# Attention in an order written out by hand: new engine orders and PSUM banks, with GpSimd's scaling and VectorE's work on weight words kept apart

## The chip, the cores and the metric

The kernel runs on one core of a Trainium2 chip. Five engines have queues of their own: TensorE (PE; its weight loads are PEld), VectorE (DVE), ScalarE (ACT), GpSimd (POOL) and SyncE (SP, which issues most DMAs). They work side by side and wait for one another by semaphores. The metric is the device time of one execution in microseconds, the lower the better.

## The reference, cut to what matters

Causal attention on 24 heads (2 batches of 12), then an ELU feed-forward, then a maxout feed-forward:

```python
scores = scale * (q @ k.T); scores = where(mask, -1e9, scores)   # (2, 12, 448, 448), head_dim 64
attn = softmax(scores); x = attn @ v                             # -> (896, 768)
h = x @ w_in; g = where(h > 0, h, exp(min(h, 0)) - 1)            # w_in (768, 2048)
x = g @ w_out                                                    # w_out (2048, 768)
h = maximum(maximum(x @ w1, x @ w2), x @ w3)                     # each (768, 768)
return (h @ w_out2).astype(float32)
```

## The kernel before, in words

The weights arrive as float64 words. Each is turned into float32 from its two 32-bit halves and then split into a high and a low part, so that one product is made of three matmuls (high by high, high by low, low by high).

Attention works on 12 pairs of heads, numbered 0 to B. Pairs 0 to 5 are the first batch (token half 0), pairs 6 to B the second (token half 1). Every step has a letter, and its digits are the pair, then the head or group:

- PE: `Q` transposes q or k (`qk_pe`, L196), `S` makes the scores (`s_pe`, L234), `T` transposes the weights of attention (`t_pe`, L297), `A` multiplies by v (`av_pe`, L322), `D` is an early part of `x @ w_in` for the first two blocks of w_in (`d_pe`, L357). The digits behind a colon are the PSUM banks (0 to 7) that the step takes.
- DVE: `M` adds the mask and takes the row maximum (`s_max`, L254), `I` adds a constant to the row sums and inverts them (`r_inv`, L280 and L281), `Y` is the low part of x (`x_lo`, L339), `f` and `k` finish the early g, and `b`, `c`, `l` work on a block of w_in: `b` shifts a word (`d_shift`, L406), `c` joins words in two instructions (`d_join`, through `join`, L99 and L100), `l` makes the low part (`d_lo`, L416).
- ACT: `E` is the exponential (`s_exp`, L268), `X` the high part of x (`x_hi`, L333), `a` and `h` work on w_in (`d_scale` L402, `d_hi` L413), `e` and `g` on the early g.
- DVE or ACT, as the table says: `K` copies transposed q or k out of PSUM (`qk_copy`), `C` copies the transposed weights (`t_copy`; L314 on DVE, L312 on ACT).
- POOL: `N` scales one piece of the weights by the inverted sum (`e_norm`, L287), four pieces to a head. A `T` step needs two to four of them.

The order is not found by a scheduler. `PLAN` (from L454) writes down, for each engine, the order of all its steps, and the loop below it issues them inside `tc.manual_schedule()` (L572), each once what it needs has been issued. On the chip an engine then works strictly through its own line and waits at each step for the results it reads and for the bank it writes. A bank is free when the step that reads it last (`holds`, L546) is done; for `A` that is the pair's `X` and `Y`.

After the table the dense part begins (L606). Its first unit is block 0 of w_in on token half 1: `h_unit(0, ...)` runs 18 matmuls (`ph`, L357) in the order of the pairs 6, 7, 8, 9, A, B, three for each: the high part of x, the low part, the high part. Then come block 1, and from block 2 on both halves; the second feed-forward follows (`py`, L723; `bx`, `by`, `bz`, L781), then the last product (L1049).

Of the kernel before, what the change touches and what calls it, by code (L numbers as in the profile page):

```python
# [31 lines left out]
def tile_attention_elu_maxout(  # L32
# [413 lines left out]
    def spin(n):  # L446
        for _ in range(n):
# [8 lines left out]
            L0 L1 L2 L3 V0 V1 R0 L4 R1 L5 V2 L6 V3 L7 V4 L8 V5 L9 R2 V6 LA V7 LB V8 V9 VA VB  # L456
            """,
        "PE": """
            Q00:0 Q01:1 S02:23 S00:45 S01:67 Q11:0 Q10:1 Q21:3 Q20:2 S11:46 S12:01 S10:57 S22:32
            S20:41 S21:05 Q31:7 Q30:3 T001:2 T002:4 T000:7 T010:5 T012:3 T011:1 S32:75 S31:34  # L460
            S30:12 A0:6 Q40:0 T100:2 Q41:3 T101:1 T111:4 T110:5 T112:0 T102:2 S42:37 S40:14
            S41:50 A1:2 T202:7 Q50:1 T201:5 Q51:0 Q61:3 T211:4 T210:5 T212:2 Q60:7 T200:3 T312:5
            T310:1 Q71:0 T300:2 T311:6 T301:4 T302:1 S52:32 S60:75 S61:60 S51:32 S50:41 A2:5
            A3:2 T410:4 Q81:6 Q70:7 T402:1 T412:0 T400:5 T401:3 T411:6 S62:75 S72:14 S71:36
            S70:75 A4:0 D00:4 T610:1 Q90:2 T511:6 D01 T512:0 T510:7 Q80:6 T611:5 T612:2 D02
            QA0:3 Q91:1 T500:0 D03 T600:7 T501:6 T502:3 T601:0 T602:7 S82:21 S81:30 S92:67
            S91:12 S90:57 S80:63 A5:0 A6:6 D04 T700:5 D05 T711:3 T710:7 T712:0 T702:2 QB0:5
            QB1:6 T701:7 T802:4 T810:5 QA1:0 T812:7 T801:2 T811:6 T800:5 SB2:04 SA2:32 SB0:16
            SA0:74 SB1:32 SA1:05 A7:1 A8:4 D10:7 T900:3 T902:0 T901:6 D11 T912:2 T910:0 T911:3
            D12 TB01:6 A9:0 D13 D14 D15 TB02:2 TB00:3 TB10:4 TA02:5 TA01:1 TA00:2 TB12:4 TB11:6  # L470
            TA11:3 TA12:7 TA10:4 AB:6 AA:2
            """,
        "DVE": """
            K00 M011 M001 M003 M000 M002 K11 M010 M013 M012 I00 M102 M100 M111 M101 M103 M113
            I01 M201 M211 M203 M212 M210 M213 C000 M110 C002 C001 M112 M202 M200 I10 M302 M310
            M313 M300 I11 M303 M312 M311 K40 K41 M301 I21 I20 C110 C112 C102 b0 M400 M410 M411
            M403 M402 M412 I31 M401 I30 M413 Y1 K61 C210 K51 Y0 C310 C200 C300 c0 M501 M511 C301
            M600 M613 M500 M510 M512 I41 M503 I40 M602 M603 M610 M513 M612 Y2 M502 b1 K70 C400
            C410 C411 M601 M611 I51 M710 M702 I61 l0 M711 M701 Y3 I50 M712 Y4 M703 I60 M713 M700
            c1 C510 K80 KA0 C600 C612 C502 C501 M811 M801 M800 M810 M911 M901 M802 M812 I71 I70  # L480
            M803 M903 M813 I80 M910 M913 Y5 M912 I81 C700 Y6 C710 M902 f0 C712 C702 C810 KA1
            C711 M900 l1 MB11 MA01 MA11 MB01 C800 MB03 MA13 I90 I91 k0 MB00 MA03 MB02 MA00 MA02
            MA10 MB13 IB0 MB12 MB10 C902 C900 C901 IA0 C910 C911 IB1 Y8 MA12 Y7 IA1 b2 CB02 CB01
            f1 CB12 CA00 CA10 CA02 CA12 k1 Y9 YB YA c2 l2
            """,
        "ACT": """
            K01 E011 E001 E003 E000 K10 E002 K21 K20 E013 E010 E012 E101 E111 E100 E113 K31 K30
            E103 C010 C012 C011 E212 E102 E210 E110 E112 E202 E200 E203 E213 C100 E211 E201 C101
            C111 E311 E310 E300 E313 E302 E301 E410 E312 E303 X0 X1 C201 C202 E413 K50 C212 C211
            a0 K60 C312 C311 K71 E411 E412 C302 E403 E401 E400 h0 E402 E500 E511 E613 E510 X2  # L490
            E600 E501 E512 K81 E513 C402 C401 E610 E612 C412 E611 E602 E503 X3 E502 E601 X4 E603
            a1 C511 K90 E712 C610 E701 C512 E703 h1 C500 E713 K91 C601 C602 E711 E710 C611 E801
            E702 E800 E901 E700 E811 E812 E802 E803 E810 X5 E813 E913 E912 X6 e0 a2 KB0 C701
            E911 KB1 C802 C801 C811 E910 C812 E900 g0 E903 EB11 E902 EB03 EA11 EA01 EA03 EB01
            EB00 EB02 EA02 EA10 EB12 EA00 X8 EB13 EB10 C912 EA13 EA12 X7 e1 CB10 CB00 CB11 g1 X9
            CA11 CA01 XB XA h2
            """,
        "POOL": """
            N001 N002 N003 N000 N012 N010 N013 N011 N101 N103 N102 N111 N112 N113 N110 N100 N201
            N200 N211 N203 N212 N210 N202 N213 N311 N312 N303 N310 N313 N302 N300 N301 N412 N411  # L500
            N413 N403 N402 N401 N410 N400 N510 N512 N613 N511 N612 N513 N500 N611 N610 N503 N600
            N603 N601 N602 N502 N501 N712 N702 N701 N710 N703 N713 N803 N802 N711 N700 N813 N801
            N810 N812 N800 N811 N911 N901 N910 N903 N900 N913 N902 N912 NB01 NB02 NB00 NB03 NA02
            NB13 NA03 NA00 NB10 NB12 NA01 NA13 NB11 NA10 NA12 NA11
            """,
    }

# [155 lines left out]
    with tc.manual_schedule():  # L663
# [375 lines left out]
        def bank4(name):  # L1039
            kinds.append(kinds.pop(0))  # L1040
            return bank3(kinds[-1], name)[:, :DMO]
# [49 lines left out]
        l1 = bank4("l1")  # L1091
# [50 lines left out]
        l2 = bank4("l2")  # L1142
# [47 lines left out]
```

## Time and profile before

| | |
|---|---|
| median of 3 runs | 481.5 us (481.31 to 481.86) |
| the profiled execution | 481.89 us |
| its span, first to last instruction | 480.1 us |
| attention: first transpose to the end of the last `A` | 4.78 to 97.87 us |
| PE busy | 473.9 us, 99% of the span |
| DVE, ACT, POOL busy | 387.5, 315.5, 50.2 us |
| granted TensorE clock | 1.000 over the span |

A row of a view has a start and a duration in microseconds, the engine, the line of the kernel, the instruction with what it writes and reads, its shape, and in brackets how long its engine had been idle and who released it. Busy time counts overlapping records once: matmuls are pipelined, and one record reaches into the next.

### The profile page before, as it was taken

To read this page: it belongs to the slowest core of one execution; us is meant where nothing else is said; L and a number is where in the kernel's file an instruction comes from. 1 tells how busy PE (TensorE), PEld (TensorE's weight loads), DVE (VectorE), ACT (ScalarE), POOL (GpSimd) and SP (SyncE) were. 2 spreads that over 40 slices of the span, in tenths; PEclk is the share of its full clock that TensorE was granted. 3 is DMA by queue.
4 is the path that set the end of the run, shared out by engine and by line. 5 is a ranking of instruction groups with operands and counts; after the bars stand their busy time and mean duration, and the time that the engine had idled before them with its cause. 6 is when DMAs were issued, how large, how long until landed. Compare 5 with 4: busy or idle time off the path is not lost.

```text
span 480.1 us, 7494 instructions
## 1 busy us (share of the span) xinstructions
PE 473.9 (99%) x2674; PEld 416.5 (87%) x2674; DVE 387.5 (81%) x757; ACT 315.5 (66%) x647; POOL 50.2 (10%) x104
## 2 busy tenths in 40 slices
PE   8999999999999999999999999999999999999997
PEld 5776777789998899988998899889999999999996
DVE  4999989768988888656776765698888878988985
ACT  4999899668998888655575745564555544535530
POOL 1673764500000000000000000000000000000000
PEclk9999999999999999999999999999999999999999
DMA  9999310027758765217775777631444432000104
GB/s 184 245 204 244 106 42 1 2 67 229 237 173 277 242 200 187 88 48 246 248 248 187 236 244 260 209 125 66 132 131 133 131 125 73 1 0 2 41 26 164
DMA packets 81653, 69.69 MB, mean 145 GB/s; under 512 B 35152, under 2 KB 75472, under 8 KB 81616
## 3 DMA queue, kind: packets, MB, share of 16 engines
q1 hardware_dynamic: 80544, 68.89, 49.3%
q8 instruction: 21, 0.34, 0.3%
q10 hardware_dynamic: 1072, 0.33, 0.3%
q14 instruction: 16, 0.13, 0.1%
HBM read 59.38 MB, written 9.83 MB: 144 GB/s over the span
## 4 chain that ended last, share of the span: by engine, by line
PE 96%; POOL 2%; DVE 1%; issue 0%; ACT 0%; POOLq 0%; DVEq 0%
PE py L723 24%; PE ph L357 24%; PE bx L781 14%; PE by L781 7%; PE s L234 5%; PE te L297 4%; PE av L322 4%; PE bz L781 3%; PE bzf L1049 3%; PE bxf L1049 2%; POOL e L287 2%; PE byf L1049 2%; PE bxl L1049 1%; PE tk L196 1%; PE tq L196 1%; PE idle L448 1%
## 5 line engine op out<-in xcount | busy, mean ns | idle before, releaser
L357 PE MATMUL ph<-x,ws_l 128*128 128x512 f32 (+2 forms) x576 | 118.6, 365 | 0.0
L723 PE MATMUL py<-gs,ws_o 128*128 128x512 f32 (+1 forms) x576 | 116.2, 363 | 0.0
L357 PEld LDWEIGHTS ph<-x,ws_l 128*128 128x128 f32 x576 | 103.9, 188 | 12.4 <-issue 1.0
L723 PEld LDWEIGHTS py<-gs,ws_o 128*128 128x128 f32 x576 | 104.3, 188 | 11.7
L287 POOL TENSOR_SCALAR e<-e,r 112x336 f32<-112x336 f32 (+3 forms) x96 | 48.9, 528 | 41.5 <-DVE r L281 40.8
L268 ACT ACTIVATE e<-e,nm 112x448 f32<-112x448 f32 (+3 forms) x96 | 49.9, 532 | 2.7 <-DVE nm L254 2.5
L254 DVE CUSTOM_DVE_ANT_0 e<-s,mask 112x224 f32<-112x224 f32 (+3 forms) x96 | 37.9, 441 | 2.4 <-PE s L234 2.3
L137 ACT ACTIVATE ws_o<-c_o 128x512 fp32r<-128x512 f32 x24 | 15.2, 632 | 36.3 <-PE py L723 36.3
L781 PE MATMUL by<-ops_s,wb 128*128 128x448 f32 x162 | 35.8, 365 | 0.0
L138 DVE TENSOR_TENSOR ws_o<-c_o,ws_o 128x512 fp32r<-128x512 f32 x24 | 16.6, 693 | 19.9 <-ACT ws_o L137 19.8
L781 PEld LDWEIGHTS by<-ops_s,wb 128*128 128x128 f32 x162 | 30.5, 188 | 2.4
L297 PE MATMUL te<-ident,e 112*112 112x112 f32 x240 | 27.5, 261 | 1.3 <-POOL e L287 1.2
L297 PEld LDWEIGHTS te<-ident,e 112*112 112x112 f32 x240 | 23.9, 134 | 3.7 <-POOL e L287 2.0
L661 ACT ACTIVATE u<-bx 128x448 f32<-128x448 f32 x9 | 4.9, 545 | 32.9 <-PE bx L781 32.9
L234 PE MATMUL s<-qk 64*112 64x224 f32 (+3 forms) x192 | 24.9, 405 | 0.2 <-ACT qk L211 0.2
L322 PE MATMUL av<-et,vn 112*64 112x448 f32 (+3 forms) x192 | 24.4, 404 | 0.0
L99 DVE SCALAR_TENSOR_TENSOR c_o<-c_o,raw_o 128x512 uint32<-128x512 uint32 x24 | 16.6, 693 | 9.5 <-ACT raw_o L95 8.7
L99 DVE SCALAR_TENSOR_TENSOR ce<-ce,raw_e 128x768 uint32<-128x768 uint32 x18 | 17.3, 958 | 7.1 <-ACT raw_e L95 7.1
L322 PEld LDWEIGHTS av<-et,vn 112*64 112x64 f32 x192 | 12.0, 137 | 12.4 <-issue 5.6
L137 ACT ACTIVATE gs<-g 128x512 fp32r<-128x512 f32 (+2 forms) x30 | 17.3, 577 | 7.6 <-DVE g L373 7.5
L234 PEld LDWEIGHTS s<-qk 64*112 64x112 f32 x192 | 16.1, 173 | 6.9 <-issue 1.5
L138 DVE TENSOR_TENSOR gs<-g,gs 128x512 fp32r<-128x512 f32 (+2 forms) x30 | 18.6, 621 | 4.1 <-ACT gs L137 4.0
(169 smaller groups left out, 870.7 us busy)
## 6 DMA issues: line engine op xcount, KB each, us to landing
raw_e<-in_moe_w_dram SPq DMA_DIRECT2D x18, 768.0 KB, 4.9
raw_l<-in_moe_w_in_dram SPq DMA_DIRECT2D x16, 768.0 KB, 5.4
raw_o<-in_moe_w_out_dram SPq DMA_DIRECT2D x24, 512.0 KB, 3.6
turned<-ce SPq DMA_DIRECT2D x18, 384.0 KB, 2.7
quad<-turned SPq DMA_DIRECT2D x18, 384.0 KB, 4.1
wx<-in_moe_w_out_dram SPq DMA_DIRECT2D x12, 384.0 KB, 3.1
qn<-in_q_dram SPq DMA_DIRECT2D x24, 112.0 KB, 4.2
vn<-in_v_dram SPq DMA_DIRECT2D x12, 224.0 KB, 4.4
```

Of the source, the lines that this page charges most:

```text
L99: nc.vector.scalar_tensor_tensor(r, r, 3, low, ALU.logical_shift_left, ALU.bitwise_or)
L138: nc.vector.tensor_tensor(lo, src, f32(hi), ALU.subtract)
L234: nc.tensor.matmul(s[j][:C, o : o + (c + 1) * C], qk[:, a, c * C : (c + 1) * C], qk[:, c2, : (c + 1) * C], start=(w == 0 and n == 0), stop ...
L254: nc.vector.tensor_tensor_reduce(out=e_t[h][:, EOFF[c] : EOFF[c] + (c + 1) * C], in0=ps_now.pop(("s", h, c)), in1=mask[:, (NCH - 1 - c) * ...
L268: nc.scalar.activation(e, e, AF.Exp, bias=nm_t[h][:, c : c + 1], scale=-1.0, accum_out=sm_t[p][:, j, c : c + 1],)
L287: nc.gpsimd.tensor_scalar(e, e, ps_now["r", h][:, c : c + 1], 1.0, ALU.mult, ALU.mult)
L297: nc.tensor.transpose(t[:C, n : n + C], e[:, EOFF[c] + j * C : EOFF[c] + (j + 1) * C], ident[:C, :C],)
L322: nc.tensor.matmul(a[j * D : (j + 1) * D, kc * C : S], vn[:, j * NCH + kc, :], et[j][:, TOFF[kc] : TOFF[kc] + S - kc * C], start=(n == 0), ...
L357: nc.tensor.matmul(ps, w(a, kc), x(c, kc), start=(i == 0), stop=(i == len(seq) - 1))
L723: nc.tensor.matmul(py[m, b][:, : at.stop - at.start], w[:, a, kc * P : (kc + 1) * P], g_sp[hk * HK + kc][:, c, at], start=(hk == 0 and i = ...
L781: nc.tensor.matmul(bank[:, :S], w, side[:, c, k, :], start=(not onto and k == 0 and (a, c) == (0, 0)), stop=(k == K2 - 1 and (a, c) == (1, ...
L1049: nc.tensor.matmul(out, a(x, k)[:, rows], b(y, k), start=begin and n == 0, stop=end and n == len(seq) - 1,)
```

## The change

Only `PLAN` changes (and one blank line goes, so that lines behind it move up by one). The steps are the same; the order of each engine but SP is new, PE's steps have other banks, and 27 copies (23 `C`, 4 `K`) go from DVE to ACT while 17 (11 `C`, 6 `K`) go the other way, so that DVE has 183 steps (193 before) and ACT 176 (166). In making the new orders, a scaling step of POOL and a step of DVE on words or blocks of weights were taken as never running at the same time. The last lines of four of the tables:

```diff
         "PE": """
...
-            D12 TB01:6 A9:0 D13 D14 D15 TB02:2 TB00:3 TB10:4 TA02:5 TA01:1 TA00:2 TB12:4 TB11:6
-            TA11:3 TA12:7 TA10:4 AB:6 AA:2
+            A7:7 A8:1 D10:6 T910:4 T900:0 T911:3 T902:2 T901:4 T912:0 D05 D11 A9:2 D12 TA01:3
+            TB10:0 TB11:4 TB12:5 D13 D14 TB02:0 TB01:4 TB00:5 D15 TA02:3 TA00:1 TA11:0 TA10:5
+            TA12:4 AB:3 AA:5
         "DVE": """
...
-            f1 CB12 CA00 CA10 CA02 CA12 k1 Y9 YB YA c2 l2
+            IB1 IB0 C910 C902 IA0 C912 f0 IA1 Y8 CB02 k0 b2 CA10 CA12 f1 k1 YB c2 l2 YA Y9 Y7
         "ACT": """
...
-            EB00 EB02 EA02 EA10 EB12 EA00 X8 EB13 EB10 C912 EA13 EA12 X7 e1 CB10 CB00 CB11 g1 X9
-            CA11 CA01 XB XA h2
+            EA11 g0 CB10 CB11 CB12 X8 CA01 CB00 X9 CB01 CA02 e1 CA11 CA00 g1 XB XA h2 X7
         "POOL": """
...
```

The first place is VectorE's join of block 1 of w_in (`c1`) about the middle of attention. Before, it stands behind the work on pairs 6 and 7, and the rows are these (`e14`, `e15` are heads of pair 7, `r12` and `et11` heads of pairs 6 and 5):

```order
L280 TENSOR_SCALAR r12_932<-sm6_704 112x4
L281 RECIPROCAL r12_932<-r12_932 112x4
L254 ISA e15_857,nm15_858<-s15_0_873,mask_79 112x448
L254 ISA nm15_858 112x1
L254 ISA e14_861,nm14_862<-s14_1_846,mask_79 112x112
L254 ISA nm14_862 112x1
L99 SCALAR_TENSOR_TENSOR c_l1_898<-c_l1_898,raw_l1_157 128x768
L100 SCALAR_TENSOR_TENSOR c_l1_898<-raw_l1_157,c_l1_898 128x768
L314 COPY et11_939<-te11_0_958 112x224
L213 TENSOR_SCALAR qk8_804<-tq8_961 128x448
```

The same place of the order after:

```order
L339 TENSOR_TENSOR x1_59<-av4_860,x0_58 128x448
L213 TENSOR_SCALAR qk9_957<-tq9_925 128x448
L213 TENSOR_SCALAR qk8_959<-tq8_933 128x448
L215 COPY qk9_957<-tk9_938 128x448
L314 COPY et13_999<-te13_2_968 112x448
L99 SCALAR_TENSOR_TENSOR c_l1_847<-c_l1_847,raw_l1_157 128x768
L100 SCALAR_TENSOR_TENSOR c_l1_847<-raw_l1_157,c_l1_847 128x768
L314 COPY et11_1032<-te11_0_1010 112x224
L254 ISA e16_1034,nm16_1035<-s16_2_1028,mask_79 112x224
```

The join no longer follows directly on the inverted sums of pair 6; it stands behind the copy of a transposed piece of pair 6 (`et13`), that is, behind a step that needs all four scalings of that head.

The second place is the end of VectorE's line and of ScalarE's in attention (`x1_59` and `x0_58` are the low and high parts of x, `av7` to `av11` the products of pairs 7 to B, `c_l2` and `ws_l2` block 2 of w_in). VectorE before:

```order
L440 TENSOR_TENSOR gs1_1526<-g_1_0_1520,gs1_1526 128x448
L339 TENSOR_TENSOR x1_59<-av9_1444,x0_58 128x448
L339 TENSOR_TENSOR x1_59<-av11_1540,x0_58 128x448
L339 TENSOR_TENSOR x1_59<-av10_1555,x0_58 128x448
L99 SCALAR_TENSOR_TENSOR c_l2_1199<-c_l2_1199,raw_l2_589 128x768
L100 SCALAR_TENSOR_TENSOR c_l2_1199<-raw_l2_589,c_l2_1199 128x768
L416 TENSOR_TENSOR ws_l2_1569<-c_l2_1199,ws_l2_1569 128x768
```

VectorE after:

```order
L440 TENSOR_TENSOR gs1_1548<-g_1_0_1544,gs1_1548 128x448
L339 TENSOR_TENSOR x1_59<-av11_1532,x0_58 128x448
L99 SCALAR_TENSOR_TENSOR c_l2_1306<-c_l2_1306,raw_l2_611 128x768
L100 SCALAR_TENSOR_TENSOR c_l2_1306<-raw_l2_611,c_l2_1306 128x768
L416 TENSOR_TENSOR ws_l2_1565<-c_l2_1306,ws_l2_1565 128x768
L339 TENSOR_TENSOR x1_59<-av10_1551,x0_58 128x448
L339 TENSOR_TENSOR x1_59<-av9_1428,x0_58 128x448
L339 TENSOR_TENSOR x1_59<-av7_1319,x0_58 128x448
```

ScalarE after, at the same place (before, the high part of pair 7 stood eight rows ahead of the high part of pair B):

```order
L436 ACTIVATE gs1_1548<-g_1_0_1544 128x448
L333 ACTIVATE x0_58<-av11_1532 128x448
L333 ACTIVATE x0_58<-av10_1551 128x448
L413 ACTIVATE ws_l2_1565<-c_l2_1306 128x768
L333 ACTIVATE x0_58<-av7_1319 128x448
```

The join and split of block 2 have moved ahead of the low parts of pairs A, 9 and 7, and pair 7 is now the last of all.

The third place is PE's step from attention to the dense part, with the semaphores that a row waits for (PE before, then PE after):

```order
L322 MATMUL av10_1555<-et20_1523,vn10_1122 64x224
L322 MATMUL av10_1555<-et21_1529,vn10_1122 64x224
L357 MATMUL ph0_0_1585<-x0_58,ws_l0_713 128x448 [waits PE_49]
L357 MATMUL ph0_0_1585<-x1_59,ws_l0_713 128x448
L357 MATMUL ph0_0_1585<-x0_58,ws_l0_713 128x448 x2
L357 MATMUL ph0_0_1585<-x1_59,ws_l0_713 128x448
L357 MATMUL ph0_0_1585<-x0_58,ws_l0_713 128x448 x2
L357 MATMUL ph0_0_1585<-x1_59,ws_l0_713 128x448
```

```order
L322 MATMUL av10_1551<-et20_1491,vn10_1137 64x224 [waits Activation_49]
L322 MATMUL av10_1551<-et21_1541,vn10_1137 64x224
L357 MATMUL ph0_0_1585<-x0_58,ws_l0_696 128x448 [waits DVE_49]
L357 MATMUL ph0_0_1585<-x1_59,ws_l0_696 128x448
L357 MATMUL ph0_0_1585<-x0_58,ws_l0_696 128x448
L357 MATMUL ph0_0_1585<-x0_58,ws_l0_696 128x448 [waits Activation_49]
L357 MATMUL ph0_0_1585<-x1_59,ws_l0_696 128x448
L357 MATMUL ph0_0_1585<-x0_58,ws_l0_696 128x448 x2
```

The order of PE's rows is the same; the first matmul of the dense part now waits for VectorE, and the fourth, which reads pair 7's high part, for ScalarE.

## Rows read from the trace of the kernel before

**Rows 1.** The page: span, then busy time of each engine.

```profile
span 480.1 us, 7494 instructions
PE 473.9 (99%) x2674; PEld 416.5 (87%) x2674; DVE 387.5 (81%) x757; ACT 315.5 (66%) x647; POOL 50.2 (10%) x104
```

**Rows 2.** Chain of waits, 98 us to the end: start, duration, engine and line.

```profile
97.87 108.79 PE ph L357 x540
206.66 116.00 PE py L723 x576
```

**Rows 3.** Windows: length, busy by engine (instructions), granted clock, DMA share, GB/s.

```profile
10.00:48.00 38.00, 37.89 (x331) 27.69 (x331) 36.60 (x154) 37.91 (x129) 20.52 (x42) 1.00 1.15 230
48.00:58.00 10.00, 8.82 (x68) 6.82 (x69) 9.22 (x28) 8.79 (x26) 8.93 (x15) 1.00 0.28 62
58.00:98.00 40.00, 40.00 (x332) 29.36 (x330) 33.91 (x120) 33.07 (x105) 19.43 (x40) 1.00 0.11 30
```

**Rows 4.** Chain of waits, 0 to 98 us.

```profile
1.19 3.60 PE idle L448 x8
4.78 0.93 PE tq L196 x4
...
6.99 2.15 PE s L234 x16
...
9.68 0.38 PE tq L196 x4
...
21.88 1.59 POOL e L287 x3
...
23.52 1.36 PE te L297 x12
...
48.67 8.27 POOL e L287 x13
...
93.95 3.92 PE av L322 x32
```

**Rows 5.** Timeline, 44 to 60 us.

```profile
53.41 1.46 DVE L99 SCALAR_TENSOR_TENSOR c_l<-c_l,raw_l 128x768 uint32<-128x768 uint32 x1
...
54.90 1.09 DVE L100 SCALAR_TENSOR_TENSOR c_l<-raw_l,c_l 128x768 uint32<-128x768 uint32 x1
...
56.98 0.40 PE L297 MATMUL te<-ident,e 112*112 112x112 f32 x2 [1.18 <-POOL e L287]
```

**Rows 6.** Timeline of POOL, 0 to 100 us.

```profile
48.67 8.69 POOL L287 TENSOR_SCALAR e<-e,r 112x448 f32<-112x448 f32 x14 [0.43 <-DVE r L281]
...
64.65 7.17 POOL L287 TENSOR_SCALAR e<-e,r 112x336 f32<-112x336 f32 x15 [0.43 <-DVE r L281]
```

**Rows 7.** Line L280, all instructions: duration in ns, min/median/max.

```profile
L280 DVE TENSOR_SCALAR r<-sm x24: 140/172/524, 11.5 to 89.0; 112x4 f32<-112x4 f32 x24
```

**Rows 8.** Timeline, 92 to 106 us.

```profile
97.80 8.49 PE L357 MATMUL ph<-x,ws_l 128*128 128x448 f32 x40
97.92 0.55 ACT L333 ACTIVATE x<-av 128x448 fp32r<-128x448 f32 x1 [1.34 <-PE av L322]
98.50 0.63 DVE L339 TENSOR_TENSOR x<-av,x 128x448 fp32r<-128x448 f32 x1 [1.26 <-ACT x L333]
99.04 0.95 DVE L99 SCALAR_TENSOR_TENSOR c_l<-c_l,raw_l 128x768 uint32<-128x768 uint32 x1
100.02 0.96 DVE L100 SCALAR_TENSOR_TENSOR c_l<-raw_l,c_l 128x768 uint32<-128x768 uint32 x1
101.01 0.85 ACT L413 ACTIVATE ws_l<-c_l 128x768 fp32r<-128x768 f32 x1 [2.55 <-DVE c_l L100]
...
101.89 0.96 DVE L416 TENSOR_TENSOR ws_l<-c_l,ws_l 128x768 fp32r<-128x768 f32 x1 [0.91 <-ACT ws_l L413]
```

**Rows 9.** Windows at the end of the span and behind it.

```profile
476.00:480.00 4.00, 0.62 (x4) 0.30 (x2) 0.36 (x1) 0.33 (x1) 0.00 (x0) 1.00 0.29 98
480.00:482.00 2.00, 0.00 (x0) 0.00 (x0) 0.00 (x0) 0.00 (x0) 0.00 (x0) 0.65 0.00 0
```

More of the change, by code (lines that the diff above doesn't have):

```diff
@@ L458, in tile_attention_elu_maxout @@
         "PE": """
[L459 to L469, printed above, removed]
-            D12 TB01:6 A9:0 D13 D14 D15 TB02:2 TB00:3 TB10:4 TA02:5 TA01:1 TA00:2 TB12:4 TB11:6
@@ L471, in tile_attention_elu_maxout @@
-            TA11:3 TA12:7 TA10:4 AB:6 AA:2
+            Q00:0 Q01:1 S02:23 S00:45 S01:67 Q11:0 Q10:1 Q20:2 Q21:3 S12:45 S11:70 S22:16 S10:23
+            S20:54 S21:70 T002:3 Q30:1 T001:6 T000:0 Q31:3 T011:1 T010:4 T012:0 S32:23 S31:65
+            S30:41 A0:0 Q40:2 Q41:5 T102:3 T110:7 T111:6 T100:4 T112:2 T101:5 S42:16 S40:47
+            S41:25 A1:3 T202:1 T201:6 Q51:7 Q60:2 T210:4 Q61:5 Q50:1 T212:3 T312:7 T311:6 T200:5
+            T301:1 T300:0 T302:4 T310:3 T211:5 S52:72 S50:04 S60:35 S61:61 S51:24 A2:0 A3:7
@@ new lines, in tile_attention_elu_maxout @@
+            T412:5 Q71:3 Q70:2 T402:1 T410:4 T411:0 T400:5 T401:3 S62:42 S72:61 S71:50 S70:42
+            A4:3 D00:5 D01 Q90:4 D02 Q80:2 Q91:0 T600:6 QA0:7 Q81:1 T612:3 T501:4 T610:7 T611:2
+            T601:6 T602:0 T500:1 T510:3 T511:4 T502:2 T512:7 S82:06 S81:12 S92:37 S80:04 S90:63
+            S91:17 A5:4 A6:2 D03 T711:0 T710:1 T712:7 QB1:6 QB0:3 D04 QA1:2 T802:0 T800:7 T702:4
+            T701:3 T810:6 T801:2 T812:1 T811:7 T700:6 SA2:03 SB2:21 SB0:47 SB1:01 SA1:32 SA0:64
+            A7:7 A8:1 D10:6 T910:4 T900:0 T911:3 T902:2 T901:4 T912:0 D05 D11 A9:2 D12 TA01:3
@@ L472, in tile_attention_elu_maxout @@
+            TB10:0 TB11:4 TB12:5 D13 D14 TB02:0 TB01:4 TB00:5 D15 TA02:3 TA00:1 TA11:0 TA10:5
+            TA12:4 AB:3 AA:5
             """,
         "DVE": """
[L474 to L483, printed above, removed]
@@ L484, in tile_attention_elu_maxout @@
-            f1 CB12 CA00 CA10 CA02 CA12 k1 Y9 YB YA c2 l2
+            K00 M001 M011 M003 M013 M012 M010 M002 M000 K21 M111 M101 I00 M112 M100 M102 M110
+            M113 I01 M201 M210 M211 M212 M213 C000 M103 M203 C010 C011 I10 C012 M302 M202 M310
+            M301 I11 M312 M311 M200 M300 M303 K40 M313 I20 C100 C112 C102 M401 I21 M411 M402
+            M413 I31 M400 M403 M410 M412 I30 Y1 K51 C201 K61 Y0 C210 b0 K60 C300 c0 M511 M513
+            M503 M501 M610 I41 M613 M502 I40 M603 M500 M512 M612 M602 M510 Y2 C412 K70 M600 C411
@@ L485, in tile_attention_elu_maxout @@
+            b1 M601 M611 C401 I50 l0 M700 I60 M702 M703 M712 I61 M713 M710 M701 Y3 I51 M711 Y4
+            K90 K80 K91 C612 c1 C510 M801 M811 M802 M901 M800 M810 M911 M813 M812 I70 I71 M902
+            M803 M900 I81 M910 I80 M912 M903 M913 Y6 C712 Y5 KB0 KB1 C710 l1 C802 C812 C811 MA01
+            MB11 MA11 MB01 MB03 MB13 I91 MB10 MB02 MB12 MA03 I90 MA00 MA12 MA13 MB00 MA02 MA10
+            IB1 IB0 C910 C902 IA0 C912 f0 IA1 Y8 CB02 k0 b2 CA10 CA12 f1 k1 YB c2 l2 YA Y9 Y7
             """,
         "ACT": """
-            K01 E011 E001 E003 E000 K10 E002 K21 K20 E013 E010 E012 E101 E111 E100 E113 K31 K30
@@ L488, in tile_attention_elu_maxout @@
[L488 to L493, printed above, removed]
@@ L494, in tile_attention_elu_maxout @@
-            E911 KB1 C802 C801 C811 E910 C812 E900 g0 E903 EB11 E902 EB03 EA11 EA01 EA03 EB01
-            EB00 EB02 EA02 EA10 EB12 EA00 X8 EB13 EB10 C912 EA13 EA12 X7 e1 CB10 CB00 CB11 g1 X9
-            CA11 CA01 XB XA h2
+            K01 E001 E011 E003 K11 K10 K20 E000 E002 E012 E010 E111 E013 E101 E100 E113 C002 K30
+            E102 K31 C001 E103 E110 E212 E210 E112 E201 E211 E213 E202 E203 E200 K41 C111 C110
+            E311 C101 E312 E301 E310 E313 E302 E303 E300 X1 C202 a0 X0 E410 K50 E413 C212 C200
@@ new lines, in tile_attention_elu_maxout @@
+            C312 E400 C302 C310 C211 C311 C301 E401 E412 E411 E402 E403 h0 E501 E610 E513 E500
+            E603 X2 E503 X3 K71 C410 C402 C400 E502 E612 E601 E600 E611 E602 E512 E613 E510 a1
+            E511 X4 E700 E702 E713 KA0 E701 C600 K81 C501 C611 C610 C602 C601 C500 C502 C512
+            C511 E710 E703 E712 E711 E810 E802 E813 E811 E801 E812 E803 E800 X5 E901 X6 E912 h1
+            C711 E900 E903 KA1 C800 E902 C810 C701 C801 C702 E913 E910 EA01 C700 E911 EB11 EB13
+            a2 EB02 EB10 EB03 EB12 EB01 EB00 EA02 EA03 C900 EA00 EA13 C911 C901 EA10 e0 EA12
@@ L497, in tile_attention_elu_maxout @@
+            EA11 g0 CB10 CB11 CB12 X8 CA01 CB00 X9 CB01 CA02 e1 CA11 CA00 g1 XB XA h2 X7
             """,
         "POOL": """
[L499 to L502, printed above, removed]
@@ L503, in tile_attention_elu_maxout @@
-            N810 N812 N800 N811 N911 N901 N910 N903 N900 N913 N902 N912 NB01 NB02 NB00 NB03 NA02
-            NB13 NA03 NA00 NB10 NB12 NA01 NA13 NB11 NA10 NA12 NA11
+            N000 N003 N002 N001 N011 N013 N012 N010 N100 N102 N101 N103 N111 N112 N113 N110 N203
+            N200 N202 N201 N213 N212 N210 N312 N311 N310 N313 N211 N301 N300 N302 N303 N413 N410
+            N401 N400 N402 N411 N412 N403 N502 N500 N603 N601 N501 N602 N611 N613 N610 N612 N503
+            N600 N512 N511 N513 N510 N701 N712 N703 N710 N711 N700 N813 N713 N802 N812 N801 N803
@@ L505, in tile_attention_elu_maxout @@
+            N810 N800 N702 N811 N910 N913 N902 N903 N912 N901 N900 N911 NB13 NB10 NB01 NB03 NA01
+            NB11 NB12 NB00 NA02 NA03 NA00 NA13 NA10 NA11 NA12 NB02
             """,
```

## The prediction

> **What bounds the kernel now.** I read the page first: PE is busy 473.9 us of a span of 480.1, DVE 387.5, ACT 315.5, POOL 50.2 [rows 1]. The question is then only where PE waits. The chain of waits from 98 us on answers for four fifths of the time: it is PE alone, stage behind stage, 540 matmuls of `ph` in 108.79 us (0.20 each), then `py` [rows 2]. The windows answer for attention: from 10 to 98 us PE is idle 0.11 us, then 1.18, then 0.00 [rows 3], together 1.29. So a microsecond that PE loses anywhere behind the start is a microsecond of the end: nothing later waits for something that would swallow it. What attention can give back is small, and what its end can cost is not limited.
>
> The chain of attention names POOL twice, for 1.59 us at 21.88 and for 8.27 us at 48.67 [rows 4]. That is not 9.9 us of waiting: PE was busy 8.82 us of the ten in which the second stands [rows 3]. The real wait there is 1.18 us, of a transpose that begins at 56.98 and waited for POOL [rows 5].
>
> **The middle of attention: what the change removes.** POOL's run of 14 scalings from 48.67 takes 8.69 us, 0.62 each; a run of 15 from 64.65 takes 7.17 us, 0.478 each [rows 6]. At the second rate the first would have ended 8.69 - 14 x 0.478 = 2.0 us sooner. In the same stretch VectorE's join takes 1.46 and 1.09 us [rows 5], and 0.95 and 0.96 at 99 us, when POOL has no work left [rows 8]: each engine is longer where both run. The new order puts this join behind the copy of a fully scaled piece of pair 6. Without it POOL is up to 2.0 us earlier, more than the 1.18 that PE waited, so this wait should go. Late next would be the many transposes that follow each other there; PE has them in a new order too. Besides, PE loses some 0.2 us at three places in front of transposes; one is the 12 that take 1.36 us at 23.52, where four take 0.38 and so 12 would take 1.15 [rows 4]. Bounds: all goes, 1.29 + 3 x 0.2 = 1.9 us gained; or the new order has as many such waits elsewhere as the old, 1.9 us of them added, so that 1.9 is lost. I take 1.3 gained, the idle time that the windows show.
>
> In one respect the change takes too little into account. The first instruction of VectorE's inversion, a tensor_scalar on 112x4 numbers, mostly takes 172 ns, but up to 524 [rows 7]; it is not work on weight words, and the new order does nothing for it. The Trainium skill ("SBUF — State Buffer", "Who interferes with whom") says that such an instruction, too, can need the port pair that VectorE shares with GpSimd, and that the engine that comes second waits until the other's instruction is over; the long ones in this trace agree with it in size. By that rule the two inversions of pair 6 could still be late by 0.35 us each, and the gain would be 0.6 instead of 1.3, the time 485.6 instead of 484.9. As the old order paid this as well, I leave the term at 1.3.
>
> **Copies.** Ten steps net go from DVE to ACT, copies of 448 columns or fewer. An instruction of ACT that reads as many from PSUM takes 0.55 us [rows 8], so ACT gets at most 5.5 us more. From 10 to 48 us it has no room, busy 37.91 of 38, from 58 to 98 it has 6.93 us [rows 3]. By the table ACT has 13 `C` steps of pairs 0 to 3 before and 14 after, and 6 `K` of pairs 0 to 4 before and 7 after: two of the ten fall in the full stretch, the rest later. Cost nothing, hidden by PE's work; if that cover is gone, the two copies, 1.1 us; both lie inside the bounds above.
>
> **The end of attention: what the change adds.** Here a row of the order decides. Before, the low parts of pairs 9, B and A stand ahead of the join and split of block 2, and the dense part begins without a pause: its first `ph` matmul starts at 97.80, the last `A` ends at 97.87 [rows 4, 8]. After, VectorE's line ends `k1 YB c2 l2 YA Y9 Y7` and ScalarE's `XB XA h2 X7`, and the second three of the 18 matmuls of the first dense unit need pair 7. More than that: the product of pair 7 (`A7:7`) is the last step to take bank 7, its bank is free only after `Y7`, and the very first dense matmul waits for VectorE. So PE does nothing between the last `A` and `Y7`.
>
> How long is that? The trace of before shows the same steps behind its last `A`, in the same sequence. From its end at 97.87: high part to 98.47, low part from 98.50, the join's two from 99.04 and from 100.02 to 100.98, ScalarE's `h2` 101.01 to 101.86, `l2` 101.89 to 102.85 [rows 8]; 4.98 us. After, the sequence hangs on the last `A` but one (`AB`), which ends half of 3.92 us, 1.96 us, earlier [rows 4]: `l2` ends 4.98 - 1.96 = 3.02 us behind the last `A`. Then come `YA`, `Y9` and `Y7`. Behind a low part the next instruction starts 0.54 us after it (98.50 to 99.04), some 0.09 before its end, and the last one takes its full 0.63 [rows 8]: 3.02 - 0.09 + 0.54 + 0.54 + 0.63 = 4.64. `X7` is no later: `h2` ends at 101.86 - 97.87 - 1.96 = 2.03 us and `X7` at about 2.6. A release takes 0.03 us (98.47 to 98.50), and the 0.07 of overlap is lost: 4.74. Bounds: without any overlap on VectorE 3.02 + 3 x 0.63 + 0.1 = 5.0; and if the first three matmuls could run ahead of the wait, 3 x 0.2 less, 4.1. I take 4.7. Nothing hides it: PE has one line, and behind the waiting matmul stand all the others. The other engines' work on block 2 is done sooner instead, but PE asks for it only two units later, and nothing shows that it waits for it now.
>
> **Sum.** 481.89 (the profiled execution, span 480.1 and 1.8 around it) + 4.7 - 1.3 = 485.3. That execution lies 0.4 above the median of 481.5, so the forecast for the median is 484.9. Its own range is 481.5 + 4.1 - 1.9 = 483.7 to 481.5 + 5.0 + 0 = 486.5.
>
> **Rivals.** First, the pause costs more than its length. At the start PE runs at the lower of its two clock levels (1.2 GHz): four transposes take 0.93 us at 4.78 and 0.38 at 9.68; scores at 6.99 already take their later time [rows 4]. At the end, PE has been idle since about 476.6, and the granted clock is 1.00 up to 480 and 0.65 on the mean of the two microseconds behind [rows 9]: left without work, PE loses the higher level. The wait of 1.18 us at 57 did not take it [rows 3, 5]; a pause of 4.7 us is longer than any that PE has between 10 us and its last matmul. If the clock falls, PE starts the dense part at half speed. What the lower level cost at the start is at most half of the time from 1.19 to 6.99, 2.9 us [rows 4]; I take 2.0: 486.9. The Trainium skill ("TensorE: Matmul & The Clock Gate", "What's actually happening") has a rule for this: an idle PE goes back to half its clock and gets it back only after a busy while; by it this rival comes true whenever the pause is long enough.
>
> Second, the middle does not get better: another wait takes the place of the one removed, as PE, ACT and DVE all have little room from 10 to 58 us. Then the end's cost stands alone or with up to 1.9 more: 486.2 to 488.1.
>
> Third, on the other side: the chain is right and the idle time wrong, and POOL's 9.86 us on it are time that PE can win back, because the matmuls on it are stretched rather than waiting. If all of it went, 481.5 - 9.9 + 4.7 = 476.3. It decides from the point where attention gains more than the 4.7 of its end. Against it: PE's transposes and scores run at the same rates around POOL's stretch as elsewhere, and only 1.29 us of idle time is there.
>
> **How the numbers follow.** Forecast 0.54; the clock falls 0.29; the middle gains nothing 0.12; the third rival, or something unseen that undoes the pause, 0.05. A measurement of this kernel tells 0.2% (about 1 us) from no change. All but the last 0.05 are slower by more than that: slower 0.95, within 0.2% 0.02, faster 0.03. The range from 483.7, the forecast's lower end, to 487.8, the clock's upper end (484.9 + 2.9), leaves out the last 0.05 and about a tenth of the rest.
>
> **What would show it.** In the profile after, the waits of PE list `ph` behind DVE's low part of x, 4 to 5 us once, right behind the last `A`; the chain goes there through L99, L100, L413, L416 and three of L339. The wait for POOL near 57 us is gone or under 0.4 us; POOL's run there is shorter per piece. The join takes 0.95 and 0.96. From the first dense matmul to the end the time is the same as before, 382.3 us (97.80 to 480.1), unless the granted clock is under 1.00 behind the pause. I am wrong if PE goes from `A` to `ph` without a pause, if attention's last `A` ends before 95 or after 99.8 us, or if the dense part's length changes with the clock at 1.00.

## The result, and the profile after

The changed kernel takes 487.24 us, median of 4 runs (486.74 to 487.53), against 481.68 us before (4 runs). The ratio is 1.0118, 95% interval 1.0106 to 1.0129: slower by 1.2%. The range (483.7 to 487.8) holds it, but the forecast of 484.9 is 2.3 us too low: what was measured is the first rival, at 486.9. The forecast's own range ended at 486.5; the rest up to 487.8 was there for that rival.

The page after (before: [rows 1]): span, then busy time of each engine. PE is 2.2 us busier with the same 2674 matmuls.

```profile
span 485.5 us, 7486 instructions
PE 476.1 (98%) x2674; PEld 419.9 (86%) x2674; DVE 382.2 (79%) x747; ACT 318.1 (66%) x657; POOL 48.7 (10%) x104
```

Who waited for whom on PE, over the whole run (microseconds in total, times, longest):

```profile
PE ph L357 <- DVE x L339: 4.7, 1, 4.7
PE idle L448 <- DVE still L574: 1.2, 1, 1.2
```

POOL is gone from this list, and one wait of 4.7 us for a low part of x has come; the other row is the start of the program and is the same before. The chain of waits from 90 us on shows where it lies:

```profile
92.27 2.06 PE av L322 x16
94.33 0.02 issue
94.35 0.55 ACT x L333
94.91 0.02 issue
94.93 0.62 DVE x L339
95.55 0.87 DVE c_l L99
96.43 0.02 issue
96.45 0.97 DVE c_l L100
97.42 0.02 issue
97.44 0.85 ACT ws_l L413
98.30 0.02 issue
98.32 0.96 DVE ws_l L416
99.28 1.61 DVE x L339 x3
100.88 0.04 issue
100.93 11.21 PE ph L357 x42
```

This is the chain of [rows 8] once more, instruction by instruction, but now hung on the last `A` but one and with three low parts behind it; PE, which ended its last `A` at 96.19, goes on at 100.93. The windows around it (columns as in [rows 3]) show what the pause did to the clock:

```profile
98.00:99.00 1.00, 0.00 (x0) 0.00 (x0) 0.68 (x1) 0.72 (x2) 0.00 (x0) 1.00 0.40 73
99.00:100.00 1.00, 0.00 (x0) 0.00 (x0) 1.00 (x3) 0.00 (x0) 0.00 (x0) 0.53 0.96 311
100.00:105.00 5.00, 4.07 (x11) 3.64 (x12) 2.39 (x4) 1.71 (x2) 0.00 (x0) 0.50 0.23 80
105.00:106.00 1.00, 1.00 (x5) 0.89 (x4) 0.40 (x1) 0.00 (x0) 0.00 (x0) 0.55 0.00 0
106.00:107.00 1.00, 1.00 (x7) 0.93 (x6) 0.00 (x0) 0.00 (x0) 0.00 (x0) 1.00 0.75 255
```

The granted clock is halved just behind 99 us and whole again near 106; for the first five microseconds of the dense part PE works at the lower level (1.2 GHz).

The middle of attention, in the window that answers to the second of [rows 3], and POOL's run there:

```profile
48.00:58.00 10.00, 10.00 (x90) 8.83 (x88) 9.42 (x32) 9.63 (x32) 8.36 (x16) 1.00 0.21 49
```

```profile
47.29 9.14 POOL L287 TENSOR_SCALAR e<-e,r 112x336 f32<-112x336 f32 x16 [4.59 <-DVE r L281]
```

PE is never idle there now. POOL's pieces take 0.571 us each (9.14 / 16), still more than the 0.478 of [rows 6], because two of the 16 are long. The first, at 47.29, takes 1.06 us beside VectorE's split of block 0; the last takes 1.28, where a piece of its size takes 0.36 at 53.25, because the join has not got quite clear of the scalings:

```profile
55.15 1.28 POOL L287 TENSOR_SCALAR e<-e,r 112x112 f32<-112x112 f32 x1
55.24 0.95 DVE L99 SCALAR_TENSOR_TENSOR c_l<-c_l,raw_l 128x768 uint32<-128x768 uint32 x1
```

What the orders took as never running at the same time still does so twice on the chip; PE no longer waits for it.

Where the 5.4 us between the two spans come from: the last `A` ends at 96.19 instead of 97.87 (-1.68); the first dense matmul starts at 100.93 instead of 97.80, so that the pause has cost 3.13 + 1.68 = 4.81; from there to the end it is 384.57 us instead of 382.30 (+2.27, the half clock).

### The profile page after: what moved, and what is told of

It is laid out like the page before. It is cut to its first block, busy times and chain, and to the rows that moved or that the text cites. A ratio compares the mean times of both kernels' runs of the same rounds, so it can differ in the third digit from the quotient of the medians.

```text
span 485.5 us, 7486 instructions
## 1 busy us (share of the span) xinstructions
PE 476.1 (98%) x2674; PEld 419.9 (86%) x2674; DVE 382.2 (79%) x747; ACT 318.1 (66%) x657; POOL 48.7 (10%) x104
## 4 chain that ended last, share of the span: by engine, by line
PE 98%; DVE 1%; ACT 0%; issue 0%
PE ph L357 25%; PE py L722 24%; PE bx L780 14%; PE by L780 7%; PE s L234 5%; PE te L297 5%; PE av L322 5%; PE bz L780 3%; PE bzf L1048 3%; PE bxf L1048 2%; PE byf L1048 2%; PE bxl L1048 1%; PE tq L196 1%; PE tk L196 1%; PE idle L448 1%; DVE x L339 0%
## 5 line engine op out<-in xcount | busy, mean ns | idle before, releaser
L357 PE MATMUL ph<-x,ws_l 128*128 128x512 f32 (+2 forms) x576 | 120.7, 369 | 4.7 <-DVE x L339 4.7
L357 PEld LDWEIGHTS ph<-x,ws_l 128*128 128x128 f32 x576 | 105.8, 191 | 17.7 <-DVE x L339 5.1
L287 POOL TENSOR_SCALAR e<-e,r 112x336 f32<-112x336 f32 (+3 forms) x96 | 47.3, 514 | 39.6 <-DVE r L281 28.0
L254 DVE CUSTOM_DVE_ANT_0 e<-s,mask 112x336 f32<-112x336 f32 (+3 forms) x96 | 37.3, 440 | 2.4 <-PE s L234 2.3
L297 PE MATMUL te<-ident,e 112*112 112x112 f32 x240 | 26.1, 260 | 0.0
L234 PE MATMUL s<-qk 64*112 64x112 f32 (+3 forms) x192 | 25.1, 405 | 0.0
L373 DVE SCALAR_TENSOR_TENSOR g<-e,ph 128x512 f32<-128x512 f32 (+2 forms) x32 | 19.7, 615 | 5.5 <-ACT e L367 5.4
L234 PEld LDWEIGHTS s<-qk 64*112 64x112 f32 x192 | 17.7, 173 | 6.2 <-issue 1.5
```

The costliest lines, as they stand in the source:

```text
L234: nc.tensor.matmul(s[j][:C, o : o + (c + 1) * C], qk[:, a, c * C : (c + 1) * C], qk[:, c2, : (c + 1) * C], start=(w == 0 and n == 0), stop ...
L254: nc.vector.tensor_tensor_reduce(out=e_t[h][:, EOFF[c] : EOFF[c] + (c + 1) * C], in0=ps_now.pop(("s", h, c)), in1=mask[:, (NCH - 1 - c) * ...
L287: nc.gpsimd.tensor_scalar(e, e, ps_now["r", h][:, c : c + 1], 1.0, ALU.mult, ALU.mult)
L297: nc.tensor.transpose(t[:C, n : n + C], e[:, EOFF[c] + j * C : EOFF[c] + (j + 1) * C], ident[:C, :C],)
L357: nc.tensor.matmul(ps, w(a, kc), x(c, kc), start=(i == 0), stop=(i == len(seq) - 1))
```

## The experiments

Each is timed against the kernel before in turns on the same chip (median of before 481.43 us beside e1 to e4, 481.76 beside e5 to e7, 481.55 beside e8 and e9). The edits show only the parts of the lines that change, with the engine or run behind a #.

### e1: the end of attention put back

```diff
-f1 k1 YB c2 l2 YA Y9 Y7        # VectorE
+f1 Y9 k1 Y7 YB YA c2 l2
-g1 XB XA h2 X7                 # ScalarE
+g1 X7 XB XA h2
```

> The changed kernel with the last steps of two lines put back in the old manner: VectorE ends f1 Y9 k1 Y7 YB YA c2 l2 and ScalarE g1 X7 XB XA h2, all else as changed. Theory (the low part of pair 7 behind the join and split of block 2 makes a pause of 4.7 us, and the pause costs another 2.5 us of half clock): the pause goes, the granted clock stays at 1.00, the time is 487.2 - 4.7 - 2.5 = 480.0 us, 1.5 under the kernel before. Rival (the new banks or the many moved copies make the dense part late, the tail only shows it): PE still waits at the first dense matmul, the time stays over 484 us.

Measured: 480.04 us, ratio to before 0.9967 (0.9955 to 0.9980), clock 1.00. The timeline at the step into the dense part:

```profile
95.44 7.79 PE L357 MATMUL ph<-x,ws_l 128*128 128x448 f32 x37
95.56 0.54 ACT L333 ACTIVATE x<-av 128x448 fp32r<-128x448 f32 x1 [1.27 <-PE av L322]
96.14 0.62 DVE L339 TENSOR_TENSOR x<-av,x 128x448 fp32r<-128x448 f32 x1 [0.98 <-ACT x L333]
```

The dense part starts without a wait. Four steps (three low parts and one high part) in another place are worth some 7 us, and the rest of the change, banks, copies and all other orders, is 1.4 us faster than the kernel before. No version with all its work in it is faster here.

### e2: the pause kept, PE given something to do

```diff
             assert len(issued) > before
+        granted.append(6)
+        idle = bank("idle2")
+        spin(20)
     attn.close()
```

> The changed kernel with 20 matmuls of 512 columns on zeros (bank 6, result unused) between the last A and the dense part, some 4.3 us at the full clock, so that PE has work in the pause but the low part of pair 7 is as late as before. Theory (length of the pause and clock are two terms, 4.7 and 2.5 us): the dense part starts at the same time, about 101 us, the granted clock stays at 1.00, the time is 487.2 - 2.5 = 484.7 us. Rival (the half clock has another cause than PE's idleness, or is only a figure of the record): 487.2 us again, the first dense unit as slow as in the changed kernel.

Measured: 484.72 us, ratio 1.0064 (1.0049 to 1.0080). The timeline (19 of the 20 matmuls on zeros are in the trace; then the dense part), and a window of 6 us whose seventh figure behind the length, the granted clock, is 1.00 where the changed kernel had 0.59:

```profile
96.13 4.49 PE L448 MATMUL idle<-still 128*128 128x512 bf16 x19
...
100.93 2.30 PE L357 MATMUL ph<-x,ws_l 128*128 128x448 f32 x10 [0.31 <-DVE x L339]
```

```profile
98.00:104.00 6.00, 5.69 (x28) 3.84 (x26) 3.07 (x5) 2.40 (x4) 0.00 (x0) 1.00 0.41 131
```

The dense part starts at 100.93 as in the changed kernel, and the time is 2.5 us less; in the traces it takes 382.3 us from there to the end (483.2 - 100.93), not 384.6. The two terms are separate: the pause has its length, and PE's idleness in it costs another 2.3 us by the traces, 2.5 by the medians.

### e3: a shorter pause

```diff
-f1 k1 YB c2 l2 YA Y9 Y7        # VectorE
+f1 k1 YB c2 YA Y9 Y7 l2
-g1 XB XA h2 X7                 # ScalarE
+g1 XB XA X7 h2
```

> The changed kernel with the low parts of pairs A, 9 and 7 between the join and the split of block 2 (VectorE ends YB c2 YA Y9 Y7 l2, ScalarE XB XA X7 h2): the pause loses ScalarE's and VectorE's split, 1.9 us, and should be 2.85 us. Theory (each us of the pause is one us of the end): 487.2 - 1.9 = 485.3 us if the clock falls in this pause too, 482.8 us if it does not. Rival (another wait holds the first dense matmul as well): the pause stays near 4.7 us.

Measured: 484.34 us, ratio 1.0060 (1.0046 to 1.0074), between the two figures that were given. PE's list, then the windows:

```profile
PE ph L357 <- DVE x L339: 2.9, 1, 2.9
```

```profile
97.00:98.00 1.00, 0.00 (x0) 0.00 (x0) 1.00 (x3) 0.46 (x1) 0.00 (x0) 1.00 0.28 31
98.00:99.00 1.00, 0.76 (x4) 0.73 (x5) 1.00 (x2) 0.00 (x0) 0.00 (x0) 1.00 0.89 292
99.00:100.00 1.00, 1.00 (x6) 0.94 (x5) 0.05 (x1) 0.00 (x0) 0.00 (x0) 0.88 1.08 383
100.00:103.00 3.00, 3.00 (x9) 2.66 (x9) 0.36 (x1) 1.71 (x2) 0.00 (x0) 0.50 0.08 27
103.00:104.00 1.00, 1.00 (x6) 0.90 (x6) 0.97 (x2) 0.25 (x1) 0.00 (x0) 0.92 0.00 0
```

The pause is the 2.9 us of the theory. The clock falls here too, but only when PE has been at work again for 1.5 us (from 98.24 to about 99.75), and it stays down for 3.4 us, not 6.8: half of 3.4 is 1.7 us, and 480.0 + 2.9 + 1.7 = 484.6.

### e7: only pair 7 moved forward

```diff
-f1 k1 YB c2 l2 YA Y9 Y7        # VectorE
+f1 k1 Y7 YB c2 l2 YA Y9
-g1 XB XA h2 X7                 # ScalarE
+g1 X7 XB XA h2
```

> The changed kernel with only pair 7 moved forward (VectorE f1 k1 Y7 YB c2 l2 YA Y9, ScalarE g1 X7 XB XA h2): bank 7 is free and pair 7's low part there before the last A ends, but the low parts of A and 9 stay behind the join and split of block 2. Theory (what PE waits for is the first low part that it needs, in the order of its 18 matmuls): ten matmuls of the first dense unit run (2.0 us), then PE waits for pair 9 until 4.15 us behind the last A, 2.1 us: 480.0 + 2.1 = 482.1 us if the clock stays up, near 483.8 if it falls as in e3_short_pause. Rival (the join and split themselves hold the dense part): a pause of 4 us or more at the first matmul, 484 us or more.

Measured: 483.49 us, ratio 1.0035 (1.0021 to 1.0049). Timeline of PE:

```profile
95.16 2.28 PE L357 MATMUL ph<-x,ws_l 128*128 128x448 f32 x10
99.71 4.47 PE L357 MATMUL ph<-x,ws_l 128*128 128x448 f32 x13 [2.26 <-DVE x L339]
```

Ten matmuls, then a wait of 2.26 us for pair 9, as expected. Join and split do not hold the dense part by themselves; what counts is which low part stands behind them. The clock fell again, just as PE took up work, for some 3.4 us:

```profile
99.75:103.00 3.25, 3.25 (x9) 2.91 (x10) 0.35 (x1) 1.72 (x2) 0.00 (x0) 0.50 0.17 60
```

### e4 and e6: the old order with its join moved

e4 moves `c1` from before `C510` to behind `C612`; e6 two steps further (ScalarE's `h1`, which works on the joined block, goes as much later):

```diff
-c1 C510 K80 KA0 C600 C612 C502 C501 M811      # VectorE, before
+C510 K80 KA0 C600 C612 c1 C502 C501 M811      # e4
+C510 K80 KA0 C600 C612 C502 C501 c1 M811      # e6
```

> The kernel before with one step of the change alone: VectorE's join of block 1 moved behind the copy of pair 6 (C600 C612 c1), ScalarE's h1 as much later; banks, copies and all other orders as before. Theory (the join and POOL's scalings exclude one another, and that made PE's wait of 1.2 us at 57): POOL's run of 14 pieces takes about 6.9 us instead of 8.7, the wait at 57 goes, the time is 481.6 - 1.2 = 480.4 us. Rival (PE waits there because the whole order has no room; POOL's length is a consequence): the wait moves to another step and the time stays within 0.3 us of 481.6.

> As e4_before_join_late, but the join two copies further back (C600 C612 C502 C501 c1), so that no bank that the next scores need waits behind it; ScalarE's h1 behind C611. Theory A (one wait, which only needs a place where nobody is behind the join): no wait of PE over 0.4 us in the middle, 481.4 - 1.2 = 480.2 us. Theory B (in the old order the 1.9 us of the join have no free place on VectorE): PE waits about as long at another step (scores or transposes of pairs 8 and 9), 481.2 to 481.8 us.

Measured: 481.62 us (ratio 1.0005, 0.9997 to 1.0014) and 481.54 us (0.9997, 0.9988 to 1.0006): no difference, so the rival of e4 and theory B of e6 hold. POOL's run in e4, then PE's waits in e4 and in e6:

```profile
48.73 7.27 POOL L287 TENSOR_SCALAR e<-e,r 112x448 f32<-112x448 f32 x14 [0.43 <-DVE r L281]
```

```profile
PE s L234 <- DVE et L314: 1.3, 1, 1.3
```

```profile
PE s L234 <- DVE nm L254: 1.0, 1, 1.0
```

POOL's run shrinks by 1.4 us, to 0.52 us a piece, and PE's wait for POOL at 57 us is gone. But a wait of nearly the same length stands a few microseconds later, at scores whose bank a copy (e4) or a mask step (e6) behind the join must free. At neither of the two places did the old order have room on VectorE for the 1.9 us of the join; other places were not tried.

### e5: the new order with its join among the scalings

```diff
-I61 M713 M710 M701 Y3 I51 M711 Y4 K90 K80 K91 C612 c1 C510      # e1
+I61 c1 M713 M710 M701 Y3 I51 M711 Y4 K90 K80 K91 C612 C510
```

> As e1_tail_early (480.0 us), with VectorE's join of block 1 put back among POOL's scalings: from behind the copy of pair 6 to directly behind the inverted sums of pair 6 (I61 c1 M713). Theory A (keeping the join apart from the scalings is what won the 1.4 us of the middle): two of POOL's pieces take 1.2 us instead of 0.5 or 0.6, PE waits for POOL by 1 us or more, 481.0 to 481.9 us. Theory B (the order as a whole won it, this step is one of many that fit): the wait is swallowed, 480.0 us, within 0.3.

Measured: 482.46 us, ratio 1.0012 (1.0003 to 1.0020): 2.4 us more than e1, or 2.1 if each is taken against the kernel before beside it, and over the range of either theory. PE's longest wait:

```profile
PE tq L196 <- DVE nm L254: 1.4, 1, 1.4
```

So the place of the join matters, but not for the reason of theory A: PE waits for VectorE's mask steps behind the join (banks of pair 7 that the transposes of pair 8 need), not for POOL. Two of POOL's pieces are as long as theory A said (1.15 and 1.33 us), but PE does not wait for them.

### e8 and e9: a join that reads one tensor

Both replace the two instructions of block 1's join by two reductions over the same words, so that block 1 of w_in is never joined; e8 in the kernel before, e9 in e5.

```diff
+if f == 1:
+    for n, x in enumerate((low, high)):
+        nc.vector.tensor_reduce(r[:, n : n + 1], x, axis=AX.X, op=ALU.max)
```

> The kernel before with all orders as they were, but VectorE's two join instructions of block 1, which read two tensors in SBUF each, replaced by two reductions over the same 768 words that read one (each about as long, 0.9 us; block 1 of w_in is left unjoined). Theory A (POOL is held up by the second SBUF input of VectorE's instructions): POOL's run of 14 pieces takes about 7.3 us instead of 8.7 and PE's wait of 1.2 us at 57 goes or moves, 480.4 us if it goes. Theory B (what counts is that VectorE is busy for 1.9 us there, and POOL's long pieces have another cause): POOL's run stays over 8.4 us, PE waits as before, 481.6 us.

> e5_join_back (482.5 us) with the same replacement in block 1's join (left unjoined). Theory A (in the new order, too, the join harms through POOL's scalings): POOL's run of 16 gets shorter and the time goes back to about 480.0 us. Theory B (there it is VectorE's own queue: the mask steps of pairs 7 stand behind the join, and PE waits for their banks): PE waits at the transposes of pair 8 as in e5_join_back, 482.2 us or more.

Measured: e8 480.14 us, ratio 0.9973 (0.9963 to 0.9984); e9 481.80 us, 1.0002 (0.9993 to 1.0011). The timelines, e8 and then e9:

```profile
48.26 7.28 POOL L287 TENSOR_SCALAR e<-e,r 112x448 f32<-112x448 f32 x14 [0.43 <-DVE r L281]
...
53.00 1.81 DVE L412 TENSOR_REDUCE c_l<-raw_l 128x1 uint32<-128x768 uint32 x2
```

```profile
49.99 1.82 DVE L412 TENSOR_REDUCE c_l<-raw_l 128x1 uint32<-128x768 uint32 x2
...
52.41 0.60 PE L196 MATMUL tq<-ident,qn 112*128 112x112 f32 x4 [1.05 <-DVE nm L254]
```

In e8 VectorE is busy for 1.8 us at the same place of the same order, at the very time POOL scales; with reductions in place of the join POOL's run is 1.4 us shorter, as in e4 where the join was elsewhere, PE no longer waits, and 1.4 us are won. In the old order it was the exclusion of the two engines. In e9 the same replacement wins only 0.7 us of e5's 2.4 (0.5 of 2.1 against the kernel before); the wait for the mask steps stays, at 1.05 us. In the new order, at that place, it is mostly VectorE's queue.

A reduction differs from a join in two ways: it reads one tensor, and it writes one number a row instead of 768. The timeline of before tells which counts, by two pairs of rows. Both VectorE instructions are a TENSOR_TENSOR that writes hundreds of columns; the first reads both inputs from SBUF, the second reads `av` from PSUM:

```profile
48.40 0.93 DVE L416 TENSOR_TENSOR ws_l<-c_l,ws_l 128x768 fp32r<-128x768 f32 x1
48.67 1.16 POOL L287 TENSOR_SCALAR e<-e,r 112x448 f32<-112x448 f32 x1 [0.43 <-DVE r L281]
...
49.81 0.45 POOL L287 TENSOR_SCALAR e<-e,r 112x224 f32<-112x224 f32 x1
49.86 0.62 DVE L339 TENSOR_TENSOR x<-av,x 128x448 fp32r<-128x448 f32 x1
```

The piece beside the first takes 1.16 us, where one of its size takes 0.63 at 53.41; the piece beside the second takes the 0.45 that its size takes elsewhere (51.70). So it is the second input in SBUF that counts, not the columns written.

## Why the prediction was right, and where it was not

**What bounds it.** Right. From the first dense matmul on, 382.3 us before and 384.6 after differ by the half clock alone: with the clock kept up (e2) it is 382.3 again. Nothing swallowed the pause.

**The end of attention.** Right in mechanism and size. The estimate of 4.74 us came from one sequence of before [rows 8], hung 1.96 us earlier, and three more steps; 4.7 us were measured. e1 shows that these steps are the cause, e7 that it is the order in which PE needs the low parts. The bank of pair 7 adds that the very first matmul waits, which itself reads nothing of pair 7.

**The clock.** Here the forecast took the wrong one of two cases. It gave 0.29 to a fall and priced it at 2.0 us; in all four runs the mean clock is 0.992, and it cost 2.3 us of span, 2.5 by e2. That was the step that failed, and it could have been read from the trace of before: it held two idle stretches, one of 1.2 us without a fall and the one at the end with it [rows 9]. There the mean of 0.65 means a fall at 480.6, when PE had been without work for some 4 us, less than the 4.7 us that were forecast. The range held the result only because the rival had been given room in it. That the Trainium skill ("TensorE: Matmul & The Clock Gate", "What's actually happening") names idleness as the cause is what e2 confirms: the same pause filled with matmuls keeps the clock at 1.00. With the clock as the likelier case the forecast would have been 486.9, and 487.2 to 487.4 with its price as measured.

**The middle.** The size was right: 1.3 us were forecast, 1.39 found by e1 (481.43 - 480.04); the profiled last `A` ends 1.68 us sooner. What goes beyond the 1.29 us of idle time agrees with the short losses in front of transposes that the prediction put into its bounds: in the trace of before, weight loads of transposes waited three times for POOL, 2.0 us together, in the one after never; this was not tested by itself. The step that explained the old wait is right as well (e8): the join's second input held up POOL, and without that POOL's run is 1.4 us shorter. The estimate of 2.0 put all that was long in that run down to the join; 0.5 us of it is the first piece, which stands beside the split of block 0 in either order. The inversions, which in one case of the prediction left only 0.6 us of the gain, are still long at times (up to 442 ns after, 524 before), and the gain was not smaller for it. Where the prediction failed is in what follows for the new order. "POOL's run there is shorter per piece" is only half true, 0.571 us against 0.621, since the join still meets the last piece; moving the join alone wins nothing (e4, e6), since it then stands before copies or mask steps that free banks. What won is the order as a whole, which has a place for the join where nobody waits for VectorE or for POOL. Which of its other parts (banks, copies) made that place was not taken apart.

**Copies.** Right to cost nothing that shows: ACT is busy 38.00 us of 38 from 10 to 48 us, and PE has no wait for it there. They were not tested by themselves.

**The rivals.** The second (nothing gained in the middle) and the third (10 us to be had from POOL's part of the chain) are excluded by e1: this order gained 1.4 us in attention, neither nothing nor more than the 4.7 of its end.

## What to carry to other kernels

An order written for one stage has an end, and what the next stage needs first belongs to its price: here the last steps, harmless inside attention, held up everything behind it. Where one engine sets the time, read the next stage's first instructions, list what each of them reads and which bank it writes, and put those producers ahead of work that is needed later. And a pause of that engine costs more than its length when the clock falls in it: in e2 work without use kept it up; useful work moved there was not tried.

## What the runs showed of the hardware

- The granted clock fell to the lower level in all three pauses of 2.26 us (e7), 2.9 us (e3) and 4.7 us (the changed kernel), and the fall came late: with 2.26 us as PE took up work again, for 3.4 us; with 2.9 us 1.5 us after that, also for 3.4 us; with 4.7 us for 6.8, of which PE worked 5.0. Waits of 1.0 to 1.4 us (before, e4, e5, e6, e9) left it at 1.00. So a part of what a short pause costs can lie behind it.
- An instruction of VectorE with two inputs in SBUF and one with a single input are very different neighbours for GpSimd: 14 scalings beside the join take 8.69 us [rows 6], beside two reductions of the same 768 words 7.28; in the traces of before and after the pieces that two such inputs held up took 1.06 to 1.28 us, where their sizes otherwise take 0.36 to 0.63, and a piece beside an instruction that reads one input from PSUM took its usual time. VectorE pays too: the join's first instruction takes 1.46 us beside them [rows 5] and 0.95 alone [rows 8].
